# First group's Q, K and V in 480, 480, 512 and 448 columns in place of 480 four times, and one more split load at the end

## The chip, the cores and the metric

The kernel runs on one core of a Trainium2 chip. The metric is the time of one execution on the device, in microseconds. The kernel before takes 623.56 us, the median of three runs (623.55 to 623.58). A core has a matrix engine (TensorE, PE in the profile, with its weight loads as PEld), a vector engine (VectorE, DVE), a scalar engine (ScalarE, ACT), GpSimd (POOL) and a queue engine (SyncE, SP) that here does nothing but issue transfers (DMAs). Matrix products accumulate in banks of PSUM and are copied to SBUF, the memory that the engines work from.

## The reference

An input `x` of 2048 tokens by 640 is normalised per token. The result goes through two branches: local dilated attention (32 heads of 20, each token looks at itself and the seven tokens 2, 4, ... 14 before it) and a feed-forward pair with SiLU between and behind. The two are multiplied and added to `x`. Cut to what matters:

```python
xn = _layernorm(x)                                   # 2048 x 640
qkv = xn @ wqkv                                      # 640 x 1920: Q, K, V of 640 columns each
logits = einsum(q, k at pos - 2*w, w = 0..7) * Dh**-0.5     # masked where pos - 2*w < 0
o = softmax(logits) . v at the same places
s = o @ wo                                           # 640 x 640
g = silu(silu(xn @ w1) @ w2)                         # 640 -> 1536 -> 640
out = x + s * g
```

All is fp32. The kernel gets fp32 accuracy from a faster product: each operand is split into a rounded high part and the remainder, and a product is three matmuls (high x high, low x high, high x low).

## The kernel before

**Groups and stages.** The tokens form four groups of 512 (g = 0 to 3; half of the sequence by parity of the position), each of four token tiles of 128. A group has two stages. `qkv_phase` makes Q, K and V in four *quarters* of eight heads: a quarter needs 160 columns each of Q, K and V from `wqkv`, five chunks (c = 0 to 4) of the model dimension, four token tiles and three products, which is 60 matmuls, each into one PSUM bank per token tile. The attention of a quarter runs on VectorE while TensorE goes on. `ffn_phase` makes the feed-forward pair (`up`, 15 matmuls of 512 columns for one of 12 blocks; `down`, 24 matmuls of 384 and 256 columns) and, from the second group on, the output projection `wo_phase` of the group before. `wo_last` is the last group's projection; there the residual `x` is loaded, multiplied and added by token tile, in two pieces of 384 and 256 columns, and stored.

**Widths of the quarters.** A PSUM bank holds 512 fp32 columns. In groups 1 to 3 each of the first three quarters takes 32 of the fourth's query columns along (`MORE = 32`), so the widths are 512, 512, 512 and 384. In group 0 all four are 480. `parts` (L468) says which columns of `wqkv` a unit takes, `width` (L489) how many they are, and `start` (L492) where they lie in a weight slot: 48 columns in (`QAT`) in group 0, else at 0. `evac_qkv` (L745) copies a bank out: K and V with L749, the query columns with L752, and the 32 borrowed ones into the fourth quarter's `Q` with L755.

**Weights.** A weight unit (one chunk of a quarter, or one block of `w1`, `w2` or `wo`) is loaded raw by `raw_load` (L546 for its equally spaced columns, L548 for the odd piece where it has one) into one of the borrowed buffers `xr` and `gate`. ACT copies it, rounded, into one of seven slots `w` (L581), and POOL (the first ten) or DVE (the rest) makes the remainder (L585). The chunks 0, 2 and 4 of each quarter are stored as halves in DRAM when first made (L589, `half_q`), and read back from there in later groups (L572). Their DRAM tile has the later groups' widths: so in group 0 the first three quarters store 480 columns, and the 96 that lack come from the fourth quarter's unit in three stores of 32 columns each. A slot is free for its next unit when TensorE has used it and its stores have landed.

**Order.** Instructions are not issued in the order of the code. `Weave.add` records each operation with its engine, an estimated duration, what it reads and writes, and a priority; `Weave.plan` lays out a schedule from these estimates with TensorE's order fixed, tries to close TensorE's gaps by adding order between other operations, and `emit` issues everything in the order found. Each engine then takes its own list strictly in that order, and so does SP with its transfers.

Of the kernel before, what the change touches and what calls it, by code (L numbers as in the profile page):

```python
# [11 lines left out]
AF = mybir.ActivationFunctionType  # L12
# [6 lines left out]
DC, FC = D // P, F // P  # L19
NQ = 4  # L20
HQ = H // NQ
CQ = HQ * DH
# [35 lines left out]
             ("th", 1, 1), ("sq", 2), ("th", 2, 0), ("hi", 5), ("th", 2, 1), ("sq", 3), ("th", 3, 0), ("th", 3, 1), ("hi", 6))  # L58
ON_POOL = 0, -1, 1, 3, -2, 4, -3, 2, 5, 6
BY_ACT = (0,)  # L60
IN_PARTS = 2
KEYS_FIRST = ((3, 0),)
KEYS_IN = 4.0
OUT_IN = 6.0
# [3 lines left out]
LENT0, LENT_PACE = -16.0, 12.0  # L68
QAT = 48
MORE = 32  # L70
OAT = 16
X_AT = 1.2, 6, 8
TILE_AT = 1, 1.5, 5, 6
# [19 lines left out]
class Weave:  # L93
# [21 lines left out]
    def add(self, eng, dur, fn, reads=(), writes=(), prio=0.0, lock=False, table=None, nbytes=0, more=0.0, late=0.0, at=0.0,  # L115
            spans=(), quick=0.0):
        o = Op()
        o.quick = quick
        o.eng, o.dur, o.fn, o.prio, o.lock, o.table, o.nbytes = eng, dur, fn, prio, lock, table, nbytes
        o.more, o.late, o.spans = more, late, spans  # L120
        o.seq, o.users, o.at, o.need = len(self.ops), [], at, 0
        before = set()
        for k in reads:
            if k in self.writer:
                before.add(self.writer[k])
        for k in writes:
            if k in self.writer:
                before.add(self.writer[k])
            before.update(self.readers.get(k, ()))
        for k in writes:  # L130
            self.writer[k] = o
            self.readers[k] = []
        for k in reads:
            self.readers.setdefault(k, []).append(o)
        before.discard(o)
        self.ops.append(o)
        for b in before:
            self.chain(b, o)
        return o
# [164 lines left out]
def local_attention_silu_ffn(ctx: ExitStack, tc: tile.TileContext, x, wqkv, wo, w1, w2, out):  # L304
# [26 lines left out]
    def tiles(name, n, shape, dtype=F32):  # L331
        return [sb.tile(shape, dtype, name=f"{name}{i}") for i in range(n)]

    ident = sb.tile([P, P], F32, name="ident")
    def small(name, *shape):
        return sb.tile([P, *shape], F32, name=name)


    M = [small("m0", T, HQ)]
    TH = [sb.tile([P, DC * TOK + OAT], F32R, name="th0")]  # L340
    mask, ST = small("mask", T, W), [small("st0", 2, 6)]
    TH.append(sb.tile([P, DC * TOK + OAT], F32R, name="th1"))
    M.append(small("m1", T, HQ))
    ST.append(small("st1", 2, 6))
    TL = tiles("tl", 2, [P, DC * TOK + 64], F32R)
    chunks = lambda tiles, at: [v[:, at:at + DC * TOK].rearrange("p (c n) -> p c n", c=DC) for v in tiles]
    OH, OL = chunks(TH, OAT), chunks(TL, OAT)
    TH, TL = chunks(TH, 0), chunks(TL, 0)
# [7 lines left out]
    Q = tiles("q", NQ, [P, T, CQ])  # L356
# [40 lines left out]
    def act(n, fn, reads, writes, prio, table=None, more=0.0, late=0.0, at=0.0, spans=()):  # L397
        return add("ACT", ac(n) + more, fn, reads, writes, prio, table=table, late=late, at=at, spans=spans)
# [9 lines left out]
    def dma(fn, reads, writes, nbytes, prio, dur=0.45, more=0.0, quick=0.0, at=0.0):  # L408
        add("SP", dur, fn, reads, writes, prio, nbytes=nbytes, more=more, quick=quick, at=at)
# [57 lines left out]
    first_q = NQ * DC  # L467

    def parts(i):


        _, q, c = units[i]
        cols = [(s * D + q * CQ, CQ) for s in range(3)]
        if i >= first_q:
            if q < NQ - 1:
                cols.append(((NQ - 1) * CQ + q * MORE, MORE))
            else:
                cols[0] = (q * CQ + q * MORE, CQ - q * MORE)
        return cols

    for u in units:
# [7 lines left out]
    def width(i):  # L489
        return sum(n for _, n in parts(i)) if units[i][0] == "q" else D  # L490

    def start(i):  # L492

        return QAT if i < first_q else 0

    raw_in = {}
    head = {}
# [1 line left out]
    def raw_tile(k):  # L499


        if k < DC:
            return "pr", k
        if k < early:
            s = (k - DC) % 6
            return ("xr", s) if s < 2 else ("g", s - 2)
        return "xr", k % 3

    def raw_load(k):
        i = fresh[k]  # L510
        u = units[i]
        n = width(i)
        of, s = raw_tile(k)
        raw_in[of, s] = k
        if of == "pr":
            r, kr = PRV[:, s * n:(s + 1) * n], [PRK[s]]
        elif of == "g":
            r, kr = G[:, s, :n], [("g", s, 0), ("g", s, CA)]
        else:
            r, kr = XR[s][:, :n], [("xr", s)]  # L520
        raws[i] = r, kr
        more = []
        if u[0] == "q":
            _, q, c = u
            cols, m, at = parts(i), 3, 0
            whole = wqkv[c * P:(c + 1) * P, :]
            src = whole.rearrange("p (s m) -> p s m", s=3)[:, :, q * CQ:(q + 1) * CQ]
            if i >= first_q:
                if q < NQ - 1:
                    odd, lies = cols[3], 3 * CQ  # L530
                else:
                    odd, lies, src, m, at = cols[0], 0, src[:, 1:], 2, cols[0][1]
                more.append((r[:, lies:lies + odd[1]], whole[:, odd[0]:odd[0] + odd[1]]))
            dst = r[:, at:at + m * CQ].rearrange("p (s m) -> p s m", s=m)
        elif u[0] == "w1":
            src = w1.rearrange("(c p) f -> p c f", p=P)[:, :, u[1] * P:(u[1] + 1) * P]
            dst = r.rearrange("p (c f) -> p c f", c=DC)
        else:
            m = wo if u[0] == "wo" else w2
            src, dst = m[u[1] * P:(u[1] + 1) * P, :], r  # L540
        if k in BY_ACT:
            add("ACT", 0.65, lambda: nc.scalar.dma_start(dst, src), [], kr, -1, nbytes=n * P * 4)
            return

        def go():
            nc.sync.dma_start(dst, src)  # L546
            for to, by in more:
                nc.sync.dma_start(to, by)  # L548
        dma(go, [], kr, n * P * 4, 1 + k if k < 2 * DC else clock[0] + 5, (0.62 if k < 2 * DC else 0.45) * (1 + len(more)))

    def raws_due(i, k):

        while rawn[0] < len(fresh) and fresh[rawn[0]] <= i + RAW_AHEAD and raw_in.get(raw_tile(rawn[0]), -1) <= k:
            raw_load(rawn[0])
            rawn[0] += 1

    def w_load():
# [5 lines left out]
        n = width(i)  # L563
        r = WR[s]
        at = start(i)
        both = r.rearrange("p (s d) -> p s d", s=2)[:, :, at:at + n]
        whi, wlo = both[:, 0], both[:, 1]
# [9 lines left out]
        if not k:  # L577
            raw_load(0)
            rawn[0] = 1
# [7 lines left out]
        if what[i] == "store":  # L587
            def keep(to, a, b, key):
                dma(lambda: nc.sync.dma_start(to, both[:, :, a:b].bitcast(F32)), [kh, kl], [key], 2 * (b - a) * P * 4,  # L589
                    due + 25)  # L590
# [4 lines left out]
            keep(kept[:, :, :n - past], past, n, ("half", u))  # L595
            for k in range(past // MORE):
                v = ("q", k, u[2])
                keep(halves[v][:, :, 3 * CQ:], k * MORE, (k + 1) * MORE, ("half", v, "more"))
        raws_due(i, k)

    def w_next(*want):

        i = used[0]
        assert units[i] == want and i < loaded[0], (units[i], want)
        used[0] += 1
        s, n, at = i % RING, width(i), start(i)
        return WR[s][:, at:at + n], WR[s][:, D + at:D + at + n], ("wh", s), ("wl", s)
# [134 lines left out]
    def q_keys(q, t):  # L742
        return [("q", q, t)] + [("q", q, t, k) for k in range(q if q == NQ - 1 else 0)]

    def evac_qkv(g, q, t, ps, kp):  # L745
        kv, qq = KV[q], Q[q]
        skip = MORE * q if g and q == NQ - 1 else 0
        n = CQ - skip
        act(2 * CQ, lambda: nc.scalar.activation(  # L749
            kv[:, :, HALO + t, :], ps[:, n:n + 2 * CQ].rearrange("p (s m) -> p s m", s=2), AF.Copy),  # L750
            [kp], [(k, q, t) for k in ("kv", "own", "val")], -1 if (g, q) in KEYS_FIRST else 0)
        act(n, lambda: nc.scalar.activation(qq[:, t, skip:], ps[:, :n], AF.Copy), [kp],  # L752
            [("q", q, t)] if skip else q_keys(q, t), 0)
        if g and q < NQ - 1:
            act(MORE, lambda: nc.scalar.activation(  # L755
                Q[NQ - 1][:, t, q * MORE:(q + 1) * MORE], ps[:, 3 * CQ:], AF.Copy), [kp], [("q", NQ - 1, t, q)], 0)

    def halo(g, q):
        h, par = groups[g]
# [184 lines left out]
    def qkv_phase(g, i, io):  # L944
# [10 lines left out]
        for q in range(NQ):  # L955
# [26 lines left out]
            for t in range(T):  # L982
                evac_qkv(g, q, t, *ps[t])
# [94 lines left out]
    def wo_last(g, i):  # L1078
# [10 lines left out]
        for t in range(T):  # L1089
            for cs in ((A,), (B,)) if t < IN_PARTS else ((A, B),):  # L1090
                at = slice(cs[0].start, cs[-1].stop)
# [153 lines left out]
    slot = 0  # L1245
    for g in range(NG):
# [3 lines left out]
        if g < NG - 1:  # L1250
            slot = other
# [30 lines left out]
```

## Time and profile before

| | |
|---|---|
| median of 3 runs | 623.56 us (623.55 to 623.58) |
| the profiled execution's own time | 624.1 us |
| its span on the core | 622.3 us |
| granted TensorE clock | 1.0 of full speed |
| first group's first stage, TensorE | to 60.85 us |
| transfers, mean rate over the span | 269 GB/s |
| transfers issued by SP's hardware queue | 52.8% of 16 engines' span |

The span runs from the first to the last event on the core, and the execution's own time holds some 1.8 us around it. A row of a timeline gives the start, the duration, the engine, the line, the operation, what is written and read with its shape, and in brackets how long the engine sat idle before it and what ended that. In a row of windows stand the stretch, its length, then the busy time and the number of instructions, the granted clock, the busy share of the transfer engines and their rate; with one engine chosen only its busy time is shown. In the waits view a row reads: engine, what it was about to do, what it waited for, and then microseconds in total, times, and the longest.

### The profile page before, as it was taken

To read this page: it belongs to the slowest core of one execution; us is meant where nothing else is said; L and a number is where in the kernel's file an instruction comes from. 1 tells how busy PE (TensorE), PEld (TensorE's weight loads), DVE (VectorE), ACT (ScalarE), POOL (GpSimd) and SP (SyncE) were. 2 spreads that over 40 slices of the span, in tenths; PEclk is the share of its full clock that TensorE was granted. 3 is DMA by queue.
4 is the path that set the end of the run, shared out by engine and by line. 5 is a ranking of instruction groups with operands and counts; after the bars stand their busy time and mean duration, and the time that the engine had idled before them with its cause. 6 is when DMAs were issued, how large, how long until landed. Compare 5 with 4: busy or idle time off the path is not lost.

```text
span 622.3 us, 9038 instructions
## 1 busy us (share of the span) xinstructions
PE 617.2 (99%) x3395; PEld 557.9 (90%) x3395; DVE 540.7 (87%) x545; ACT 272.7 (44%) x496; POOL 114.8 (18%) x165
## 2 busy tenths in 40 slices
PE   9999999999999999999999999999999999999997
PEld 7888999998889998999888999989988999999997
DVE  6599899999788998998948499899996999899834
ACT  5445555364545225453545521625654272252220
POOL 5800000011110142111221015121222211111100
PEclk9999999999999999999999999999999999999999
DMA  9999999599999999965999999998499999987552
GB/s 297 305 319 317 323 377 364 220 326 269 278 298 309 331 237 321 272 198 140 203 219 262 344 363 330 295 230 252 137 225 286 240 321 304 295 241 243 189 191 86
DMA packets 105114, 167.39 MB, mean 269 GB/s; under 512 B 36605, under 2 KB 66781, under 8 KB 105069
## 3 DMA queue, kind: packets, MB, share of 16 engines
q1 hardware_dynamic: 78573, 87.08, 52.8%
q0 software_dynamic: 25952, 79.31, 46.6%
q8 instruction: 27, 0.44, 0.3%
q10 hardware_dynamic: 544, 0.41, 0.2%
q14 instruction: 18, 0.15, 0.1%
HBM read 107.91 MB, written 34.16 MB: 228 GB/s over the span
## 4 chain that ended last, share of the span: by engine, by line
PE 98%; DMA 0%; DVE 0%; issue 0%
PE acc L1016 22%; PE acc L1018 15%; PE acc L973 10%; PE acc L971 10%; PE acc L972 10%; PE rot L1144 9%; PE rot L1145 9%; PE rot L1143 9%; PE acc L909 2%; PE rot L644 1%; DMA xin<-in_A_x_dram 0%; PE rot L893 0%; PE rot L1129 0%; DVE st L878 0%; PE rot L852 0%; DVE gate L1097 0%
## 5 line engine op out<-in xcount | busy, mean ns | idle before, releaser
L1016 PE MATMUL acc<-w,sh 128*128 128x384 f32 x384 | 113.4, 334 | 0.0
L971 PE MATMUL acc<-w,th 128*128 128x512 f32 (+2 forms) x300 | 112.9, 376 | 0.0
L973 PE MATMUL acc<-w,th 128*128 128x512 f32 (+2 forms) x300 | 112.8, 376 | 0.0
L972 PE MATMUL acc<-w,tl 128*128 128x512 f32 (+2 forms) x300 | 112.8, 376 | 0.0
L1018 PE MATMUL acc<-w,sh 128*128 128x256 f32 x384 | 107.3, 279 | 0.0
L792 DVE TENSOR_TENSOR pr<-q,kv 128x2560 f32<-128x2560 f32 x32 | 90.3, 2822 | 16.0 <-DMA kv<-kv 15.7
L826 DVE TENSOR_TENSOR pr<-q,kv 128x2560 f32<-128x2560 f32 x32 | 94.5, 2954 | 0.7
L1143 PE MATMUL rot<-th,w 128*128 128x512 f32 x240 | 94.2, 393 | 0.0
L1145 PE MATMUL rot<-th,w 128*128 128x512 f32 x240 | 93.8, 391 | 0.0
L1144 PE MATMUL rot<-tl,w 128*128 128x512 f32 x240 | 93.7, 391 | 0.0
L795 DVE TENSOR_REDUCE l<-pr 128x128 f32<-128x2560 f32 x32 | 90.1, 2815 | 0.3
L1156 ACT ACTIVATE sh<-rot 128x512 fp32r<-128x512 f32 x48 | 28.8, 600 | 139.7 <-PE rot L1145 139.5
L572 POOL DMA_DIRECT2D w<-half_q x52 | 37.4, 719 | 234.4 <-DVE pr L831 97.2
L572 POOL DMA_DIRECT2D w<-half_w x72 | 38.6, 536 | 202.7 <-PE acc L1018 87.9
L831 DVE TENSOR_TENSOR pr<-pr 128x1280 f32<-128x1280 f32 x64 | 74.0, 1156 | 1.3
L1018 PEld LDWEIGHTS acc<-w,sh 128*128 128x128 f32 x384 | 72.2, 188 | 1.1 <-DVE gate L1048 0.3
L1016 PEld LDWEIGHTS acc<-w,sh 128*128 128x128 f32 x384 | 72.1, 188 | 0.9
L972 PEld LDWEIGHTS acc<-w,tl 128*128 128x128 f32 x300 | 56.3, 188 | 8.8
L973 PEld LDWEIGHTS acc<-w,th 128*128 128x128 f32 x300 | 56.3, 188 | 8.7
L971 PEld LDWEIGHTS acc<-w,th 128*128 128x128 f32 x300 | 56.3, 188 | 8.7
L1016 PE MATMUL acc<-w,sl 128*128 128x384 f32 x192 | 57.9, 333 | 0.0
L749 ACT ACTIVATE kv<-acc 128x320 f32<-128x320 f32 x64 | 27.5, 441 | 60.9 <-PE acc L973 59.5
(115 smaller groups left out, 1037.8 us busy)
## 6 DMA issues: line engine op xcount, KB each, us to landing
w<-half_w POOLq DMA_DIRECT2D x72, 640.0 KB, 6.6
w<-half_q POOLq DMA_DIRECT2D x39, 512.0 KB, 5.5
half_w<-w SPq DMA_DIRECT2D x24, 640.0 KB
kv<-kv SPq DMA_DIRECT2D x15, 560.0 KB
w<-half_wo POOLq DMA_DIRECT2D x10, 640.0 KB, 8.0
kv<-kv SPq DMA_DIRECT2D x15, 420.0 KB
gate<-in_B_w_dram SPq DMA_DIRECT2D x16, 320.0 KB
w<-half_q POOLq DMA_DIRECT2D x13, 384.0 KB, 7.6
```

Of the source, the lines that this page charges most:

```text
L572: add("POOL", 1.0, lambda: nc.gpsimd.dma_start(both, src), [("half", u), ("half", u, "more")], [kh, kl], due + 10, nbytes=2 * n * P * 4)
L792: dve(2560, lambda t=t: nc.vector.tensor_tensor(out=PR, in0=win(qq[:, t:t + 2, :], W, 0), in1=win(kv[:, 0, t:t + 2, :], W, CQ), op=OP.mult ...
L795: dve(2560, lambda t=t: nc.vector.tensor_reduce(out=l[:, t:t + 2].rearrange("p t w h -> p (t w h)"), in_=PR.rearrange("p t w (h d) -> p (t ...
L826: dve(2560, lambda t=t, v=v: nc.vector.tensor_tensor(out=PR.rearrange("p t w (h d) -> p t (w h) d", d=DH), in0=e[:, t:t + 2].rearrange("p ...
L971: nc.tensor.matmul(o, hi, wh, start=c == 0, stop=False)
L972: nc.tensor.matmul(o, lo, wh, start=False, stop=False)
L973: nc.tensor.matmul(o, hi, wl, start=False, stop=c == DC - 1)
L1016: nc.tensor.matmul(a[t][0][:, :CA], st, w[:, :CA], start=first, stop=last)
L1018: nc.tensor.matmul(b[t // 2][0][:, h * CB:(h + 1) * CB], st, w[:, CA:], start=first and h == 0, stop=last, skip_group_check=True)
L1143: nc.tensor.matmul(h, wh[:, cs], TH[i][:, c, :], start=c == 0, stop=False)
L1144: nc.tensor.matmul(h, wh[:, cs], TL[i][:, c, :], start=False, stop=False)
L1145: nc.tensor.matmul(h, wl[:, cs], TH[i][:, c, :], start=False, stop=c == DC - 1)
```

## The change

The first group's third quarter takes 32 of the fourth's query columns along, so that its width is 512 and the fourth's 448. `SLOT` renumbers the places: the third quarter's 32 columns are the first of the fourth's 160, the first and second quarter's (from group 1 on) come behind them. `start` now puts units at 48 only for the first two quarters, and the third and fourth lie at 0. A stored third quarter is whole when stored, and the fourth quarter's unit has two 32-column stores to make in place of three. Apart from that `IN_PARTS` goes from 2 to 3: in `wo_last` the residual of three token tiles, not two, is loaded in two pieces.

```diff
-IN_PARTS = 2
+IN_PARTS = 3
@@
 MORE = 32
+SLOT = 1, 2, 0
@@ parts
         cols = [(s * D + q * CQ, CQ) for s in range(3)]
-        if i >= first_q:
-            if q < NQ - 1:
-                cols.append(((NQ - 1) * CQ + q * MORE, MORE))
-            else:
-                cols[0] = (q * CQ + q * MORE, CQ - q * MORE)
+        if q == NQ - 1:
+            gone = MORE * (NQ - 1 if i >= first_q else 1)
+            cols[0] = (q * CQ + gone, CQ - gone)
+        elif i >= first_q or q == NQ - 2:
+            cols.append(((NQ - 1) * CQ + SLOT[q] * MORE, MORE))
         return cols
@@ start
-        return QAT if i < first_q else 0
+        return QAT if i < 2 * DC else 0
@@ raw_load
-            if i >= first_q:
+            if len(cols) > 3 or q == NQ - 1:
@@ evac_qkv
-        skip = MORE * q if g and q == NQ - 1 else 0
+        skip = MORE * (q if g else 1) if q == NQ - 1 else 0
@@
-        if g and q < NQ - 1:
+        if q < NQ - 1 and (g or q == NQ - 2):
+            slot = SLOT[q]
             act(MORE, lambda: nc.scalar.activation(
-                Q[NQ - 1][:, t, q * MORE:(q + 1) * MORE], ps[:, 3 * CQ:], AF.Copy), [kp], [("q", NQ - 1, t, q)], 0)
+                Q[NQ - 1][:, t, slot * MORE:(slot + 1) * MORE], ps[:, 3 * CQ:], AF.Copy), [kp], [("q", NQ - 1, t, slot)], 0)
```

The change adds two lines near the top, so a line number is up to two higher after it than before. TensorE's list has the same instructions in the same order; only the widths of 120 matmuls differ. The other engines' lists move in a few places.

SP's queue while the first group's second quarter is being made; `xr` and `gate` are the raw buffers, `kv_93` the first quarter's keys and values, which are shifted between partitions. Before:

```order
L546 DMA xr_108<-in_A_wqkv_dram 128x3x160
L767 DMA kv_93<-kv_93 112x2x480
L767 DMA kv_93<-kv_93 14x2x480
L546 DMA gate<-in_A_wqkv_dram 128x3x160 x2
L546 DMA xr_107<-in_A_wqkv_dram 128x3x160
L546 DMA gate<-in_A_wqkv_dram 128x3x160
L775 DMA carry_121<-kv_93 2x2x640
L546 DMA gate<-in_A_wqkv_dram 128x3x160
```

After:

```order
L549 DMA xr_108<-in_A_wqkv_dram 128x32
L769 DMA kv_93<-kv_93 112x2x480
L769 DMA kv_93<-kv_93 14x2x480
L547 DMA gate<-in_A_wqkv_dram 128x3x160
L549 DMA gate<-in_A_wqkv_dram 128x32
L547 DMA gate<-in_A_wqkv_dram 128x2x160
L549 DMA gate<-in_A_wqkv_dram 128x128
L547 DMA xr_107<-in_A_wqkv_dram 128x2x160
L549 DMA xr_107<-in_A_wqkv_dram 128x128
L547 DMA gate<-in_A_wqkv_dram 128x3x160
L549 DMA gate<-in_A_wqkv_dram 128x32
```

Each load of the third quarter (128x3x160) is followed by its 32 columns, each of the fourth's is two transfers (128x2x160 and 128x128), and the third quarter's last chunk, the load before the last row, now stands behind two units of the fourth.

ACT around the fourth quarter's evictions (`kv_96` and `q_100` from the banks `acc`) and the first SiLU pair (`sh_84` and `sf` from `rot_119`); `w_75` to `w_81` are the seven weight slots. Before:

```order
L749 ACTIVATE kv_96<-acc_116 128x2x160
L752 ACTIVATE q_100<-acc_116 128x160
L581 ACTIVATE w_79<-gate 128x640
L581 ACTIVATE w_76<-gate 128x640
L1156 ACT_TABLE_LOAD
L1156 ACTIVATE sh_84<-rot_119 128x512
L1157 ACTIVATE sf<-rot_119 128x512
L581 ACTIVATE w_78<-xr_108 128x640
```

After:

```order
L582 ACTIVATE w_76<-gate 128x640
L582 ACTIVATE w_79<-gate 128x640
L750 ACTIVATE kv_96<-acc_113 128x2x160
L753 ACTIVATE q_100<-acc_113 128x128
L750 ACTIVATE kv_96<-acc_114 128x2x160
L753 ACTIVATE q_100<-acc_114 128x128
L750 ACTIVATE kv_96<-acc_115 128x2x160
L753 ACTIVATE q_100<-acc_115 128x128
L750 ACTIVATE kv_96<-acc_116 128x2x160
L753 ACTIVATE q_100<-acc_116 128x128
L582 ACTIVATE w_78<-xr_108 128x640
L1158 ACT_TABLE_LOAD
```

The copies into slots 76 and 79 moved from behind the evictions to ahead of them, and the one into slot 78 from behind the first SiLU pair to ahead of it.

## The prediction

> **What bounds the kernel now.** I read the page first (busy shares, then the chain that ended last), then the waits of TensorE's weight loads, then TensorE's groups by shape, and last the stretches in which one shape runs alone.
>
> ```profile
> PE 617.2 (99%) x3395; PEld 557.9 (90%) x3395; DVE 540.7 (87%) x545; ACT 272.7 (44%) x496; POOL 114.8 (18%) x165
> PE 98%; DMA 0%; DVE 0%; issue 0%
> PEld rot L865 <- POOL ident masks.py:199: 1.4, 1, 1.4
> PEld acc L1018 <- DVE gate L1048: 0.3, 1, 0.3
> ```
>
> TensorE is busy for 617.2 of 622.3 us and is 98% of the chain. Past the start its weight loads wait for another engine only for some tenths of a microsecond. So the time is the sum of the spacings of 3395 matmuls, and an edit on another engine matters only where it makes TensorE wait. A matmul's own duration (about 380 ns) overlaps the next one's, so the price of one is the distance from start to start, which I take from stretches with one shape:
>
> ```profile
> L971 PE MATMUL acc<-w,th 128*128 128x480 f32 x60 | 22.7, 378 | 0.0
> 21.97:34.93 12.96, 12.96 (x62) 1.00 1.08 276
> 34.93:47.89 12.96, 12.96 (x62) 1.00 1.08 317
> 47.89:60.85 12.96, 12.96 (x62) 1.00 1.10 316
> 296.80:337.64 40.84, 40.84 (x182) 33.78 (x181) 29.71 (x25) 19.85 (x46) 10.59 (x15) 1.00 1.32 218
> 337.64:348.07 10.43, 10.43 (x62) 10.39 (x61) 8.33 (x11) 6.02 (x15) 0.00 (x0) 1.00 1.20 296
> ```
>
> In a group's first stage each quarter is 60 matmuls (5 chunks of the model dimension, 4 token tiles, 3 products; the counts in brackets include neighbours that reach into the stretch). The first three windows are quarters 2, 3 and 4 of the first group: 12.96 us / 60 = 216.0 ns at 480 columns. The fourth is three quarters of the third group: 40.84 / 180 = 226.9 ns at 512. The fifth is its last quarter: 10.43 / 60 = 173.8 ns at 384. The granted clock is 1.00 in all of them.
>
> **The change part by part.** *Widths.* The number of matmuls and of columns stays (480 + 480 + 512 + 448 = 4 x 480), so a cost proportional to columns changes nothing. But the three widths aren't on a line: from 384 to 512 it rises by (226.9 - 173.8) / 128 = 0.415 ns a column, which puts 480 at 213.6, and 480 costs 216.0, 2.4 ns above it. The change takes 120 matmuls off that width: 60 go to 512, whose price stands in the rows, and 60 to 448, a width that the trace lacks. Its bounds: above, 216.0, since 32 columns fewer shouldn't cost more; below, as far under the line as 480 is over it, 200.4 - 2.4 = 198.0. I take the line, 200.4, since both its ends are measured and it lies between; the chord from 384 to 480 would give 201.9. The sum for quarters 3 and 4 is 60 x (226.9 + 200.4 - 2 x 216.0) = -0.28 us, with ends of -0.43 (198.0) and +0.65 (216.0).
>
> The Trainium skill, in TensorE: Matmul & The Clock Gate, section Back-to-back issue gap, gives a warm matmul a gap of its columns / 2.4 plus 2.5 ns. That is a line in the columns, and by it the sum is zero: it speaks against the change. The trace has its slope (0.415 against 1 / 2.4 = 0.417) but a larger constant (13.5 ns at 512), and at 480 it leaves the line.
>
> *Loads and stores in SP's queue.* Each of the third quarter's five weight loads gets a second transfer of 32 columns, each of the fourth's is split in two, and three of the nine 32-column stores go away: 7 issues more.
>
> ```profile
> 11.11 0.93 SPq L548 DMA_DIRECT2D xr<-in_A_wqkv_dram  x1
> 24.55 1.10 SPq L546 DMA_DIRECT2D xr<-in_A_wqkv_dram  x1
> 27.36 1.45 SPq L546 DMA_DIRECT2D gate<-in_A_wqkv_dram  x2
> 32.53 2.18 SPq L589 DMA_DIRECT2D half_q<-w  x3
> 33.32 0.61 ACT L581 ACTIVATE w<-gate 128x480 fp32r<-128x480 f32 x1 [1.70 <-DMA gate<-in_A_wqkv_dram]
> 37.43 0.61 ACT L581 ACTIVATE w<-gate 128x480 fp32r<-128x480 f32 x1 [0.68 <-DMA half_q<-w]
> 45.51 0.38 PE L972 MATMUL acc<-w,tl 128*128 128x480 f32 x1
> ```
>
> A second issue costs 0.93 us at most (L548's row) and about 0.6 otherwise. The one that is latest in PE's sense is the last chunk of the third quarter. By the order it now stands behind three 32-column issues of its quarter and four transfers of the fourth's, so it is issued some 4 to 5 us later, near 33 us. A load issued at 27.36 was there at 33.32, so this one lands near 39; with its copy on ACT (0.61) and its remainder on DVE, even behind one 2.8 us product, it is ready by 43.5. TensorE comes to it at 34.93 + 48 x 0.227 = 45.8 us (45.3 before, just ahead of the last row). About 2 us are left: nothing on the path, and each microsecond beyond them would be one of TensorE's. DVE, which takes these in a fixed order, may come out of it some 2 us late.
>
> ```profile
> 74.82 0.82 DVE L585 TENSOR_TENSOR w<-gate,w 128x640 fp32r<-128x640 f32 x1 [1.99 <-ACT w L581]
> 152.51 0.68 DVE L694 TENSOR_TENSOR tl<-turn,th 128x512 fp32r<-128x512 f32 x1
> 155.79 0.39 PE L972 MATMUL acc<-w,tl 128*128 128x512 f32 x1
> ```
>
> That lateness has a wait of 1.99 us at 74.82 to disappear in; what comes through would meet the second group's last input chunk, done at 153.19 and read at 155.79, with 2.6 us to spare. Nothing.
>
> *Evictions.* Four ACT copies of 32 columns more, 0.20 us each by this row, and the fourth quarter's are 32 columns shorter. ACT is at 44%; nothing by itself.
>
> ```profile
> 488.26 0.20 ACT L755 ACTIVATE q<-acc 128x32 f32<-128x32 f32 x1
> 62.59 0.74 ACT L581 ACTIVATE w<-gate 128x640 fp32r<-128x640 f32 x1 [0.29 <-DMA half_q<-w]
> 64.65 0.60 ACT L1156 ACTIVATE sh<-rot 128x512 fp32r<-128x512 f32 x1
> 65.14 0.59 ACT L1157 ACTIVATE sf<-rot 128x512 f32<-128x512 f32 x1
> 65.62 0.74 ACT L581 ACTIVATE w<-xr 128x640 fp32r<-128x640 f32 x1
> 67.69 0.39 PE L1143 MATMUL rot<-th,w 128*128 128x512 f32 x1
> ```
>
> *ACT's new order.* Five copies of feed-forward weights now stand ahead of the fourth quarter's evictions, and the copy that ran at 65.62 stands ahead of the first SiLU pair. Each waits until its slot's stores have landed, and ACT takes nothing past it. Late next would be the pair (64.65 and 65.14, done at 65.73): TensorE reuses its bank at 67.69, so 1.96 us of cover stand there. The stores are also issued earlier by the new order, since three fell out. I cost it at nothing and keep the loss as a rival.
>
> *Third output tile's residual in two loads.*
>
> ```profile
> 548.31 21.96 SPq L1092 DMA_DIRECT2D xin<-in_A_x_dram  x6
> 590.70 0.33 SPq L1072 DMA_DIRECT2D pr<-in_A_x_dram  x1
> 614.45 0.56 DVE L1097 TENSOR_TENSOR gate<-acc,gate 128x384 f32<-128x384 f32 x1 [1.21 <-PE acc L1016]
> ```
>
> Six issues become seven. They are over by 570.27, 20 us ahead of SP's next, and the tile is first touched at 614.45, where DVE waits for TensorE and not for a load: nothing. The orders that the planner changed near 505 us move two remainders of the attention output earlier and put one SiLU remainder behind them; all have their TensorE readers after 510 us, as before.
>
> *The sum* is -0.28 us. Against the profiled execution: span 622.3 to 622.0. The median of the runs, 623.56, lies 1.26 above that span, and this offset stays: 623.56 - 0.28 = 623.28, say **623.3 us**.
>
> **The rivals.**
>
> ```profile
> 375.99:387.04 11.05, 11.01 (x74) 10.75 (x73) 10.98 (x11) 2.19 (x3) 7.35 (x9) 1.00 1.08 353
> 397.25:407.58 10.33, 10.33 (x73) 10.33 (x72) 10.19 (x7) 4.08 (x5) 1.59 (x3) 1.00 1.17 226
> 374.33 3.14 DVE L1048 TENSOR_TENSOR gate<-acc,gate 128x384 f32<-128x384 f32 x6
> ```
>
> (1) *The one inner wait goes.* Two stretches of the same 72 matmuls take 11.05 and 10.33 us; the first holds the 0.3 us wait for L1048 of the waits view, and after it the spacing stays wider to the stretch's end. L1048 ran from 374.33 to 377.47 behind an unbroken row of DVE work. If a shifted load brings that work 0.3 us forward, the whole 0.72 goes: 623.3 - 0.7 = 622.6. Against it: nothing in the third group is edited, and DVE there hangs on events that move along with TensorE.
>
> (2) *Columns are all that counts,* the excess at 480 being carried over to the new pair: if 448 costs 216.0 x 2 - 226.9 = 205.1, within its bounds, the sum is zero and the time 623.56. For it: two of three prices do lie where a line would have them. Against it: the only odd width measured is the one that is left.
>
> (3) *Slower: ACT's head of line at 62 to 68 us.* The copy that now precedes the SiLU pair needs the fourth quarter's 32-column stores of its slot. Those are issued by 61.75 at the latest before; with a landing of 4.9 us (issued 32.53, waited for until 37.43) that is 66.6, then copy 0.74, table load 1.28 and the pair 1.1: 69.8 against TensorE's 67.69, a stall of 2.1 us. It decides from the point where SP's additional issues push these stores past about 59.7 us. Halfway, 1.0 us, gives 623.3 + 1.0 = 624.3; the full price 625.4. For it: SP's queue is the one that the change lengthens. Against it: the stores move forward in SP's order.
>
> **How the numbers follow.** Forecast 0.60, (1) 0.10, (2) 0.12, (3) 0.18. The likeliest gives 623.3, by its own bounds 623.1 to 623.5. The range takes in (1) at its foot and (3) halfway, **622.5 to 624.6**; left out are the dear half of (3) and what nobody listed. A change of 0.2%, 1.25 us, is what the measurement can surely tell from none, that is under 622.31 or over 624.81. Below needs (1) and something besides: 0.05. Above needs more than 1.5 us of (3), or 448 at its upper end together with (3): 0.09. Within: 0.86.
>
> **What would show it.** In the profile after: quarters 3 and 4 of the first group as stretches of 13.6 us at 512 columns and 12.0 at 448 (25.64 against 25.92), the second quarter still 12.96; 448's spacing near 200 ns decides between the forecast and (2). The wait for L1048's like still there near 377 with the wide spacing behind it; if it is gone, (1). No wait of TensorE between 43 and 70 us; one on a bank that the SiLU pair frees near 67.5 would be (3). The last DVE pair of the tail still released by TensorE. The forecast is wrong if 448 costs over 204 ns, or if TensorE stalls by over 0.3 us where it doesn't in the trace of before.

## The result, and the profile after

| | before | after |
|---|---|---|
| median of 10 runs each, taken side by side | 623.62 us | 627.31 us |
| lowest and highest | 623.44, 624.48 | 624.97, 630.34 |
| the profiled execution's own time | 624.1 us | 626.98 us |
| its span | 622.3 us | 625.1 us |

The ratio is 1.0058, with a 95% interval of 1.0045 to 1.0072: the change makes the kernel slower by 0.6%. The forecast was 623.3, in a range of 622.5 to 624.6. Here and below a median is over all runs, while a ratio leaves out the few slow ones, which took over 1.5% more than the fastest of their kernel (two in e3, one in each of e1, e6 and e11, two of the kernel before).

The page of the kernel after, its busy shares and the first line of its chain of waits:

```profile
PE 616.9 (99%) x3395; PEld 557.1 (89%) x3395; DVE 538.0 (86%) x545; ACT 271.7 (43%) x500; POOL 114.6 (18%) x165
PE 90%; DMA 4%; SPq 2%; DVE 1%; ACT 1%; issue 0%; ACTq 0%; DVEq 0%
```

TensorE is as busy as before (616.9 against 617.2 us), so its work hasn't become dearer. But the chain was 98% PE and is 90% now: some stretches of it run through transfers, SP and ACT. The waits of TensorE's weight loads, after, say where they come out (what it was about to do, what it waited for, us in total, times, longest):

```profile
PEld rot L1145 <- ACT sf L1159: 2.1, 1, 2.1
PEld rot L867 <- POOL ident masks.py:199: 1.4, 1, 1.4
PEld acc L973 <- ACT q L757: 1.4, 1, 1.4
PEld rot L895 <- DVE xin L885: 0.9, 2, 0.7
PEld acc L911 <- ACT w L582: 0.5, 1, 0.5
```

The second row is the start, which was there before. The first and the third are new, and both end with ACT: one on a bank that the first SiLU pair frees (L1159), one on a bank that the third quarter's evictions free (L757). The row for L1048 near 377 us has gone. Stretches of the kernel after, TensorE alone (stretch, length, busy time and instructions, granted clock, share of the transfer engines, GB/s):

```profile
22.30:35.26 12.96, 12.96 (x62) 1.00 0.93 244
35.26:48.90 13.64, 13.64 (x61) 1.00 0.89 271
48.90:62.32 13.42, 12.43 (x62) 1.00 1.02 300
62.32:74.52 12.20, 10.56 (x47) 1.00 1.04 310
379.46:389.80 10.34, 10.34 (x74) 1.00 1.10 408
```

They are the first group's quarters 2, 3 and 4, its first three `up` blocks, and the stretch that took 11.05 us before. The one of them that the prediction doesn't show of the kernel before is that of the three blocks:

```profile
60.85:71.10 10.25, 10.25 (x47) 1.00 0.98 273
```

| stretch | before | after | difference |
|---|---|---|---|
| start to quarter 2 | 21.97 | 22.30 | +0.33 |
| quarter 2 (480 columns) | 12.96 | 12.96 | 0 |
| quarter 3 (480, now 512) | 12.96 | 13.64 | +0.68 |
| quarter 4 (480, now 448) | 12.96 | 13.42 | +0.46 |
| three `up` blocks | 10.25 | 12.20 | +1.95 |
| the stretch at 377 to 390 | 11.05 | 10.34 | -0.71 |

The sum is +2.7 of the span's +2.8 us. Without its stall quarter 4 would be shorter than before by about 0.8 us (it takes 12.16 in e7 below, which has none), and so the two stalls carry the loss of this execution: some 1.3 us in quarter 4 and 1.95 us in the `up` blocks.

**The first stall.** Rows of the timeline of the kernel after: SP issuing the last chunk of the fourth quarter (slot 80), ACT's copy of it with the third quarter's evictions behind, and TensorE.

```profile
42.70 0.97 SPq L547 DMA_DIRECT2D gate<-in_A_wqkv_dram  x1
43.72 2.19 SPq L549 DMA_DIRECT2D gate<-in_A_wqkv_dram  x1
...
50.02 0.58 ACT L582 ACTIVATE w<-gate 128x448 fp32r<-128x448 f32 x1 [5.73 <-DMA gate<-in_A_wqkv_dram]
50.50 0.42 ACT L750 ACTIVATE kv<-acc 128x320 f32<-128x320 f32 x1
...
51.01 0.20 ACT L757 ACTIVATE q<-acc 128x32 f32<-128x32 f32 x1
...
51.26 0.47 PE L973 MATMUL acc<-w,th 128*128 128x448 f32 x1 [0.99 <-ACT q L757]
```

The same places in the timeline of the kernel before:

```profile
38.25 0.97 SPq L546 DMA_DIRECT2D gate<-in_A_wqkv_dram  x1
...
45.54 0.61 ACT L581 ACTIVATE w<-gate 128x480 fp32r<-128x480 f32 x1 [4.36 <-PE acc L973]
46.15 0.44 ACT L749 ACTIVATE kv<-acc 128x320 f32<-128x320 f32 x1
```

The copy into slot 80 stands on ACT ahead of the third quarter's evictions in both kernels. Before, its load was issued at 38.25 and had long landed when the copy came up: what released the copy was TensorE. After, nine more transfers stand ahead of it in SP's list (five pieces of the third quarter, four of the fourth), so it is issued 4.45 us later, and it has a second piece itself, issued at 43.72 and landed just before 50.02. The evictions start 4.35 us later than before, and TensorE, which wants the first of those banks at 51.26 - 0.99 = 50.27, finds it full.

**The second stall.** The chain of the kernel after in order of time (start, us, what), from the store of slot 76 to TensorE:

```profile
56.43 5.58 DMA half_q<-w
...
62.08 0.75 ACT w L582
...
62.85 0.83 DVE w L586
63.69 0.09 SPq L547
...
63.82 3.86 DMA half_q<-w
...
67.75 0.74 ACT w L582
...
68.51 1.28 ACT L1158
...
69.81 0.60 ACT sh L1158
70.40 0.50 ACT sf L1159
...
70.95 0.50 PE rot L1145
```

Read it upwards. TensorE waits for the SiLU pair, the pair for the copy into slot 78 ahead of it on ACT, the copy for the last 32-column store of slot 78 (issued 63.82, landed 67.68). Ahead of that store on SP stands a raw load (L547), which went out when DVE had done with its buffer; DVE had waited for the copies at 62.08, and these for a store of slot 76 (issued 56.43). In this chain two landings stand in a row, tied together by one load. The load's wait is only a small part of the lateness, though: the whole row took 0.66 us on SP (63.11 to 63.77), and e6 below has the same stall with a load there that waits for nothing. Before, SP had all stores of slot 78 in one row, over by 61.75:

```profile
59.06 2.69 SPq L589 DMA_DIRECT2D half_q<-w  x4
```

### The profile page after: what moved, and what is told of

Same layout as the page of the kernel before. It is cut to its first block, busy times and chain, and to the rows that moved or that the text cites. A ratio compares the mean times of both kernels' runs of the same rounds, so it can differ in the third digit from the quotient of the medians.

```text
span 625.1 us, 9052 instructions
## 1 busy us (share of the span) xinstructions
PE 616.9 (99%) x3395; PEld 557.1 (89%) x3395; DVE 538.0 (86%) x545; ACT 271.7 (43%) x500; POOL 114.6 (18%) x165
## 4 chain that ended last, share of the span: by engine, by line
PE 90%; DMA 4%; SPq 2%; DVE 1%; ACT 1%; issue 0%; ACTq 0%; DVEq 0%
PE acc L1018 22%; PE acc L1020 15%; PE rot L1145 8%; PE rot L1146 8%; PE rot L1147 8%; PE acc L975 8%; PE acc L974 8%; PE acc L973 8%; PE acc L911 2%; DMA half_q<-w 2%; DMA kv<-kv 1%; DMA gate<-in_A_wqkv_dram 1%; SPq L547 1%; DMA pr<-in_A_wqkv_dram 1%; PE rot L645 1%; ACT w L582 1%
## 5 line engine op out<-in xcount | busy, mean ns | idle before, releaser
L973 PE MATMUL acc<-w,th 128*128 128x512 f32 (+3 forms) x300 | 113.0, 377 | 1.0 <-ACT q L757 1.0
L975 PE MATMUL acc<-w,th 128*128 128x512 f32 (+3 forms) x300 | 112.8, 376 | 0.0
L974 PE MATMUL acc<-w,tl 128*128 128x512 f32 (+3 forms) x300 | 112.8, 376 | 0.0
L794 DVE TENSOR_TENSOR pr<-q,kv 128x2560 f32<-128x2560 f32 x32 | 90.3, 2821 | 10.2 <-DMA kv<-carry 5.4
L828 DVE TENSOR_TENSOR pr<-q,kv 128x2560 f32<-128x2560 f32 x32 | 91.8, 2870 | 0.7
L1145 PEld LDWEIGHTS rot<-th,w 128*128 128x128 f32 x240 | 45.1, 188 | 10.8 <-ACT sf L1159 2.1
```

The costliest lines, as they stand in the source:

```text
L794: dve(2560, lambda t=t: nc.vector.tensor_tensor(out=PR, in0=win(qq[:, t:t + 2, :], W, 0), in1=win(kv[:, 0, t:t + 2, :], W, CQ), op=OP.mult ...
L828: dve(2560, lambda t=t, v=v: nc.vector.tensor_tensor(out=PR.rearrange("p t w (h d) -> p t (w h) d", d=DH), in0=e[:, t:t + 2].rearrange("p ...
L973: nc.tensor.matmul(o, hi, wh, start=c == 0, stop=False)
L974: nc.tensor.matmul(o, lo, wh, start=False, stop=False)
L975: nc.tensor.matmul(o, hi, wl, start=False, stop=c == DC - 1)
L1145: nc.tensor.matmul(h, wh[:, cs], TH[i][:, c, :], start=c == 0, stop=False)
```

## The experiments

Each line gives the medians, those of the kernel before from runs on the same chip. The ratio is an estimate from the runs with its interval, and not the quotient of the two medians. "Near 50" and "near 70" are TensorE's waits in the one profiled execution of each, as the weight loads show them; another execution of the same kernel can have others.

| kernel | median, us | before there | ratio (95% interval) | near 50 | near 70 |
|---|---|---|---|---|---|
| e1: before, residual in three tiles | 624.75 | 623.77 | 1.0008 (0.9988 to 1.0029) | 0 | 0 |
| e2: after, residual in two tiles | 626.67 | 623.77 | 1.0041 (1.0025 to 1.0057) | 0 | 2.5 |
| e8: before, no offset of 48 | 624.10 | 623.77 | 1.0002 (0.9991 to 1.0013) | 0 | 0 |
| e3: after, evictions first | 627.85 | 624.03 | 1.0042 (1.0018 to 1.0066) | 0 | 2.4 |
| e4: after, SiLU pair first | 625.38 | 624.03 | 1.0014 (0.9997 to 1.0031) | 0 | 0 |
| e5: after, both first | 625.27 | 624.03 | 1.0021 (1.0001 to 1.0040) | 0 | 0.3 |
| e6: after, one load a chunk | 625.74 | 624.03 | 1.0008 (0.9991 to 1.0026) | 0 | 1.9 |
| e7: e5 and e6 together | 623.96 | 623.77 | 0.9999 (0.9990 to 1.0008) | 0 | 0 |
| e9: before, split loads | 625.89 | 624.06 | 1.0043 (1.0025 to 1.0061) | 1.0 | 0.7 |
| e11: before, ACT's new order | 633.10 | 623.63 | 1.0103 (1.0051 to 1.0155) | 0 | 0 |
| e12: after, stores ahead of loads | 625.57 | 623.97 | 1.0036 (1.0009 to 1.0063) | 1.8 | 0 |
| e13: e6 and e12 together | 623.77 | 623.70 | 1.0002 (0.9993 to 1.0011) | 0 | 0 |

### Which part of the change it is

e1 is the kernel before with the residual's part alone; e2 is the kernel after without it.

```diff
 e1, on the kernel before
-IN_PARTS = 2
+IN_PARTS = 3
 e2, on the kernel after
-IN_PARTS = 3
+IN_PARTS = 2
```

> The kernel before with the third residual tile in two loads and nothing else of the change. Theories A and B: 623.6, no difference. Rival C (the split of the last loads costs it): about 627.

> The changed kernel with the residual loads as before (two tiles in pieces): the widths alone. Theories A and B: 625 to 630 as the whole change, median near 627.3. Rival C: 623.5.

e2 keeps the loss (+2.9 us) and the wait on the SiLU pair, the longest in this list; e1 shows neither wait. So the widths' part carries it. The wait near 50 us is absent from e2's profile, although SP's list up to there is that of the kernel after: its copy into slot 80 starts at 48.06, in place of 50.02. So the first stall is not in every execution. e1's own median lies 1.0 above that of before, its interval includes none, and what takes longer in its profile is the part behind the start of the last matmul (4.66 us to the span's end, 3.83 before). With three tiles too that part takes 3.8 us in the kernel after and in e4, and 4.2 in e7 and e13, which lie level with the kernel before; so a price of some tenths is neither shown nor excluded.

e8 asks whether 480 columns are dear because they lie 48 columns into their slot.

```diff
-QAT = 48
+QAT = 0
```

> The kernel before with the first group's weights at 0 in their slots and not 48 columns in; no engine's order changes. It asks whether the 2.4 ns by which 480 columns lie above the line belong to the width or to the place. Width: the second to fourth quarters stay at 216.0 ns a matmul (12.96 us each), time 623.6. Place: 213.6 ns, 12.82 us each, and about 0.5 us less in all.

Its quarters 2 to 4 take 39.00 us from 22.54 to 61.54, 39.00 / 180 = 216.7 ns a matmul, against 216.0 with the offset: the 2.4 ns above the line belong to the width and not to its place.

### ACT's order

The next three put back the order of before on ACT, at one place or at both: the copy into slot 80 behind the third quarter's evictions and those into 76 and 79 behind the fourth's (e3), the copy into slot 78 behind the first SiLU pair (e4), and both (e5).

```diff
 e3, in evac_qkv, behind the last eviction of a quarter
+        if g == 0 and t == T - 1:
+            for k in {2: (19,), 3: (22, 25)}.get(q, ()):
+                wv.chain(last, head["hi", k])
 e4, in the up blocks, behind the SiLU pair
+        if g == 0 and f == 0:
+            wv.chain(pair, head["hi", 24])
```

> The changed kernel, with one order more: ACT's copy of the fourth quarter's last weight chunk comes behind the third quarter's evictions and not ahead of them. Theory A (ACT takes its list in order, so evictions and the SiLU pair stand behind weight copies that wait for transfers): the wait of 1.35 us near 50 us is gone, the one near 69 us stays, some 626.0 us. Theory B (SP's longer queue is the cause by itself, whoever stands where on ACT): TensorE waits all the same, for the weights themselves at about 58 us, and the time stays near 627.3.

> The changed kernel, with ACT's feed-forward weight copies put behind the fourth quarter's evictions (two of them) and behind the first SiLU pair (one). Theory A: the wait near 69 us (2.0 us) is gone, the one near 50 us (1.25 us) stays: some 625.3 us. Theory B: the stores that the copies wait for are as late as before, TensorE then waits for the weights of the second and third feed-forward blocks, and the time stays near 627.3.

> The changed kernel with both orders of the two experiments beside it. Theory A: no wait of TensorE between 40 and 75 us, 623.4 us where the wait near 377 us is still there and 622.7 where it is not; the spread of the runs shrinks from 5 us to under 1. Theory B: 626 or more.

Neither single theory held. e3's profile has no wait near 50 (its evictions start at 47.05, with no copy ahead of them), but its time is no better than that of the kernel after. Its waits view:

```profile
PEld rot L1148 <- ACT sf L1162: 2.4, 1, 2.4
```

The end of the second stall is set by the stores and not by TensorE: TensorE goes on at 69.97, in place of 70.95, so 1.0 us is won there, but as it comes earlier it waits longer, and in this execution the clock fell behind the longer wait (last section) and took the gain back. e4 takes that wait away and lies 1.35 us over the kernel before, in place of 3.69, near the 625.3 that its theory A gave; e5 lies no further down (1.24), where theory A gave 623.4 or less and theory B 626. Their profiles show only waits of 0.3 to 0.7 us, near 68 us and in the stages behind. But both profiled executions are among the fastest two of their twelve (624.01 and 624.59), and e4's shows no wait near 50, where nothing of its edit reaches; what their usual run waits for isn't seen. The order of ACT is therefore a part of it, and not shown to be all.

### SP's queue

e6 loads each chunk of the fourth quarter in one transfer, with 32 query columns that nobody uses: five issues fewer, and every other engine's list is that of the kernel after. e7 adds e5's order.

```diff
 e6, in raw_load
-            if len(cols) > 3 or q == NQ - 1:
+            if q == NQ - 1 and i < first_q:
+                r = wide_raw(of, s)
+                raws[i] = r[:, 3 * CQ - n:], kr
+            elif len(cols) > 3 or q == NQ - 1:
```

> The changed kernel with the fourth quarter's five weight loads as one transfer of 3 x 160 columns each, in place of 2 x 160 and 128; 32 of the query columns are then loaded and not used. ACT's and DVE's orders stay as they are, SP issues five transfers fewer. Theory A alone (the order costs it whatever SP does): 627.3, both waits as they are. Theory B: the last chunk lands some 2 us earlier, the wait near 50 us is gone or under 0.3 us, the one near 69 us shrinks by 1 us or more: 624 to 625.5.

> The changed kernel with the fourth quarter's weights in one transfer and with ACT's evictions and SiLU pair ahead of the weight copies: both remedies. Theories A and B: 622.6 to 623.4, no wait of TensorE between 40 and 75 us. If the widths themselves cost something that the two waits hide, over 623.6.

e6's profile has no wait near 50, as its load lands earlier (the copy into slot 80 starts at 48.64 in place of 50.02), and keeps the other one:

```profile
PEld rot L1151 <- ACT sf L1165: 1.9, 1, 1.9
```

From its chain (start, us, what): the load ahead of slot 78's last store on SP, that store until it has landed, and the copy that waits for it:

```profile
61.13 0.57 SPq L553
61.75 4.42 DMA half_q<-w
66.32 0.74 ACT w L588
```

The load goes out right behind the store before it (done at 61.02), without a wait, and the store behind it still lands only at 66.17; in e2, with its stall of 2.5, it is the same (load 60.68, store 61.48, landed 66.42). So the blocked load of the kernel after isn't needed for the second stall.

e7 has neither wait, and its time is that of the kernel before (its expectation gave 622.6 to 623.4; the gain of the widths and the missing wait near 377 us don't show in its median). As it has no stall, its quarters 2, 3 and 4 give the clean price of the widths:

```profile
21.86:34.82 12.96, 12.96 (x62) 1.00 1.08 271
34.82:48.44 13.62, 13.62 (x62) 1.00 1.06 300
48.44:60.60 12.16, 12.16 (x62) 1.00 1.09 329
```

13.62 / 60 = 227.0 ns at 512 columns and 12.16 / 60 = 202.7 at 448; together 25.78 us against 25.92 before, 0.14 less.

e9 asks the opposite: the kernel before, its widths and its order on every other engine, with the third and the fourth quarter's chunks loaded in two transfers each, which is ten issues more.

```diff
 e9, in raw_load
+            if 2 * DC <= i < first_q:
+                more.append((r[:, :CQ], whole[:, q * CQ:(q + 1) * CQ]))
+                src, m, at = src[:, 1:], 2, CQ
```

> The kernel before, all widths 480 and its order on ACT, DVE and POOL, but the first group's third and fourth quarters load each weight chunk in two transfers (K and Q or two thirds of it, then the rest): SP gets 10 issues more, nothing else changes. Theory 'both are needed' (a later landing costs only where ACT has put a copy that waits for it ahead of work that TensorE waits for): the one copy that stands ahead of the third quarter's evictions in this order too may be late, so at most a wait near 50 us, and none at 68 to 72 us, where the SiLU pair stays ahead of the copy into slot 78: 623.6 to 624.9. Theory 'SP alone' (the longer queue is enough, whatever ACT's order): the wait of some 2 us near 70 us appears here as well, 625.5 to 627. Theory 'the width of 448' (columns, not issues): nothing, 623.6 with no wait at all.

It costs 1.8 us, more than "both are needed" allowed; "SP alone" had the time right, but its wait of 2 us near 70 is 0.7 here. The waits of its weight loads:

```profile
PEld acc L974 <- ACT q L755: 1.0, 1, 1.0
PEld rot L1146 <- ACT sf L1160: 0.7, 1, 0.7
```

Both waits appear with no width changed and no row of ACT moved: the order of before has copies ahead of the third quarter's evictions (slot 80) and of the SiLU pair (76 and 79) too. They had cost nothing because what they wait for was early.

e11 tries ACT's order alone, on the kernel before.

```diff
 e11, the copies into slots 76 and 79 ahead of the fourth quarter's first eviction
+        if g == 0 and (q, t) == (NQ - 1, 0):
+            for k in (22, 25):
+                wv.chain(head["hi", k], first)
 and the copy into slot 78 ahead of the pair
+        if g == 0 and f == 0:
+            wv.chain(head["hi", 24], pair)
```

> The kernel before, with its widths and its loads, but ACT's order is made that of the change at two places: the copies into slots 76 and 79 ahead of the fourth quarter's first eviction, the copy into slot 78 ahead of the first SiLU pair. SP's list is the same up to the fourth quarter's shifts; behind them some transfers of the next stages change places. In the kernel before the copy into slot 78 ran at 65.62, right behind the pair, without a wait. Theory 'each of the two alone costs its part' (SP's queue 1.3 to 1.8 us, ACT's order some 1.7): a wait of 1 to 2 us near 69 us on the bank that the SiLU pair frees, 624.8 to 625.8, and nothing near 50 us. Theory 'SP alone' (a copy ahead costs nothing as long as its stores land as early as before): a wait of 0.5 us at most, 623.6 to 624.3.

Its median, 633.10, says nothing on the question, since the planner moved much of the later program as well, and the waits that came of it (2.9, 1.9 and 1.8 us) lie behind 180 us. Its profile does say something. ACT's timeline:

```profile
61.84 1.61 ACT L581 ACTIVATE w<-gate 128x640 fp32r<-128x640 f32 x2
...
65.08 0.60 ACT L1162 ACTIVATE sf<-rot 128x512 f32<-128x512 f32 x1
65.58 0.73 ACT L581 ACTIVATE w<-xr 128x640 fp32r<-128x640 f32 x1
66.21 0.59 ACT L1159 ACTIVATE sh<-rot 128x512 fp32r<-128x512 f32 x1
```

All three copies start without a bracket, that is without waiting, the one into slot 78 ahead of the pair's `sh`, and TensorE has no wait from 40 to 78 us. With stores as early as before (SP has all eight of slots 78 and 80 in one row from 59.15), a copy at this place costs nothing. It isn't quite the change's order: the planner put the pair's `sf` ahead of that copy, and three of the four tiles' evictions ahead of the other two.

### The two places in SP's list

`head` now also keeps the stores and the raw loads as they are recorded (25, 5 x `DC`, is the load for slot 79). e12 leaves the kernel after its number of issues and the copy into slot 78 ahead of the pair, and puts the stores of slots 76 and 78 on SP ahead of the next stage's raw loads. e13 adds e6's single loads. Neither ties an instruction of ACT to a place; the copy into slot 79 moves behind the pair together with its load.

```diff
 e12, behind the first SiLU pair
+        if g == 0 and f == 0:
+            for key in [key for key in head if key[0] == "kept" and key[1] in (3 * DC, 3 * DC + 2)]:
+                wv.chain(head[key], head["raw", 5 * DC])
```

> The kernel after, with its widths, its number of issues and its copy into slot 78 ahead of the first SiLU pair, but in SP's list the stores of slots 76 and 78 (chunks 0 and 2 of the fourth quarter) are put ahead of the next stage's raw loads, in place of one load in the middle of each; the copy into slot 79 moves behind the pair with its load. Theory 'two landings in a row' (in the change a raw load waits for the buffer that the copy into slot 76 empties, that copy waits for a store to land, and the last store of slot 78 stands behind that load on SP): the stores of 78 land by about 66 us, the copy into 78 runs without a long wait, and TensorE's wait near 69 us falls from 2.1 to under 0.7 us; what is near 50 us stays; 624.5 to 626.0. Theory 'the copy's place on ACT is enough': the wait stays at some 2 us, 626.5 to 627.5.

> The kernel after with SP's list mended in both places and ACT's list left as in e12_stores_first, no instruction of ACT pinned: the fourth quarter's weight chunks of the first group are loaded in one transfer each (160 query columns, of which 128 are used), 5 issues fewer, and the stores of slots 76 and 78 stand ahead of the next stage's raw loads. Theory 'SP is all of it': no wait above 0.5 us near 50 us or near 69 us, 623.4 to 624.4, the kernel before within its measurement. Theory 'ACT's order has a price of its own': at least one of the two waits stays, 625 to 626.

The waits of e12, the first row:

```profile
PEld acc L973 <- ACT q L757: 1.8, 1, 1.8
```

and its copy into slot 78 with the pair behind it, on ACT:

```profile
64.95 0.74 ACT L582 ACTIVATE w<-xr 128x640 fp32r<-128x640 f32 x1 [1.35 <-DMA half_q<-w]
...
67.50 0.59 ACT L1159 ACTIVATE sf<-rot 128x512 f32<-128x512 f32 x1
```

The copy still stands ahead of the pair. It starts at 64.95 in place of 67.75, the pair is done at 68.1, and no wait near 70 is left; the one near 50 is, as expected. The last 32-column store of slot 78 has landed by 64.95, in place of 67.7. In e13 both are gone. Its windows and the copy into slot 80:

```profile
35.00:48.50 13.50, 13.50 (x61) 1.00 1.05 308
48.50:61.00 12.50, 12.50 (x63) 1.00 1.05 315
61.00:72.00 11.00, 11.00 (x52) 1.00 1.04 288
```

```profile
48.14 0.58 ACT L588 ACTIVATE w<-gate 128x448 fp32r<-128x448 f32 x1 [5.43 <-DMA gate<-in_A_wqkv_dram]
```

TensorE is busy without a gap through all three. That copy still waits for its load, but ends 1.9 us earlier than in the kernel after, and that is enough. The four kernels form a square; the differences of their medians to the kernel before, in us:

| over the kernel before | load and store as in after | stores ahead of the loads |
|---|---|---|
| two loads a chunk | after: +3.69 | e12: +1.60 |
| one load a chunk | e6: +1.71 | e13: +0.07 |

By these the late load costs some 1.5 to 2.0 us, the stores behind the loads 1.6 to 2.1, and together they are the loss: e13's runs, from 623.63 to 624.94, lie level with those of before. How the loss divides is not settled. The ratios, times 623.6, give +3.6, +2.2, +0.5 and +0.1 for the same four, which is 2.1 to 3.1 for the load and 0.4 to 1.4 for the stores. The figure of e6 is the loosest: three of its twelve runs took 623.9 to 624.0 us, as if they had no stall, and its interval includes none. That the single load is needed beside the order of the stores is shown by e12, whose interval lies above 1. That the order of the stores is needed beside the single load rests on e6's median and on the wait of 1.9 in its profile.

## Why the prediction was wrong, by its own steps

**Widths.** Right in sign and in kind: 448 has a price of its own off the line's proportion, and the pair is cheaper. It was mis-sized: 448 costs 202.7 ns and not 200.4. It lies 2.4 ns above the line, just as 480 does, so half of the gain of 0.28 was there (0.14), which no median here could tell from none. Rival (2), 205.1, is off by as much on the other side.

**Loads and stores in SP's queue: the step that failed.** It said that the latest chunk "in PE's sense is the last chunk of the third quarter", and for that chunk its numbers held. Rows of the kernel after, its issue and its copy:

```profile
33.70 0.58 SPq L547 DMA_DIRECT2D gate<-in_A_wqkv_dram  x1
...
39.95 0.63 ACT L582 ACTIVATE w<-gate 128x512 fp32r<-128x512 f32 x1 [0.85 <-DMA half_q<-w]
```

Near 33 and near 39 were forecast (the copy waited last for a store, so the load had landed by then). But the step asked only when TensorE needs a chunk. The fourth quarter's last chunk isn't needed before 58 us, and so was passed over; its copy, though, stands on ACT ahead of the third quarter's evictions, which TensorE needs at 50.3. The shape of this trap was in the trace of before, where the copy at 45.54 is followed by the evictions at 46.15. Counting seven issues more also hid that ten of them come before this point and the three that fall out only behind it. e6, e9 and e13 show it.

**ACT's new order: cost at nothing, wrongly.** The mechanism was listed as rival (3), with its place right (the copy into slot 78 ahead of the pair) and its price near: 2.1 us forecast, 2.1 seen on the weight load and 1.64 as TensorE's idle time before the matmul. What sent it to the rivals was the sentence "the stores move forward in SP's order". Three stores do fall out, but of slot 78's three the last now stands behind a raw load, where before nothing stood between them, and SP comes to the three later (61.13 against 59.06): the last was issued at 63.82, where before it was out by 61.75. What was counted was rows, and not when SP comes to those that stay. The rival's own sum said more than was made of it: stores issued at 61.75, as late as before, already gave the full 2.1 us, and the term was nothing only if they came by 59.7, for which no row stood. e6 is just that case, with the store issued at 61.75 and a wait of 1.9. e12 and e13 show that the stall goes when the stores stand ahead of the loads, with the copy still ahead of the pair, so the copy's place alone isn't the cause; e11's trace agrees. How much of the lateness comes from the load's own issue, from its data on the way or from its wait isn't separated.

**What nobody listed** is that the two come together. Rival (3) at its full price gave 625.4; in the profile after, the first stall makes the rest. That the range reached to only half of (3) left it short as well.

**Rival (1)** came true in the profile after (10.34 us where there were 11.05) and takes back 0.7 us. The wait is also absent from e1, e8 and e9, which have the widths of before, and present in e5 (0.3), which has those of the change; so the widths don't decide it, and what does is open. In e5 the same 72 matmuls take 10.63 us: there the wait costs its 0.3 and no more, so the wider spacing behind it in the kernel before isn't its consequence as such, as the rival had it.

**The rest.** The evictions and the residual's third tile were costed at nothing, and no run shows a price clear of the noise. The wait of 0.5 us on the first quarter's weights (L911) and the +0.33 us at the start were not followed up; in the experiments that wait reaches from nothing to 0.7.

## What to carry to other kernels

An issue added to a queue has to be followed to every instruction that stands behind whatever waits for it, on each engine that takes its list in order: a chunk that TensorE needs late can be the one that holds up an eviction that it needs soon. In a reordered list of transfers look at what now stands ahead of a store that some engine waits for, and when the store was out before; that fewer stores are left says little. And two stalls of this kind hide each other: mending the first alone (e3) made the wait at the second longer, so try the repairs together before one of them is called useless.

## What the runs showed of the hardware

In three profiles a wait of TensorE cost more than its length. In e2 the wait on the SiLU pair left TensorE idle from about 67.5 to 69.7, and its windows then read:

```profile
70.00:72.00 2.00, 2.00 (x7) 0.59 1.12 226
72.00:74.00 2.00, 2.00 (x7) 0.55 1.05 230
74.00:76.00 2.00, 2.00 (x14) 1.00 1.12 260
```

The granted clock was 0.55 to 0.59 for some 3.5 us, with starts of the 512-column matmuls 427 ns apart in place of 227: about eight matmuls, 1.6 us on top of the wait. The same is seen in e3 behind its wait of 2.4 (0.50 from 72 to 74 us) and in e11 behind that of 2.9 (0.50 from 220 to 222). In the kernel after, the wait of 2.1 left no such mark (1.00 throughout), nor did e12's of 1.8 and e6's of 1.9. On the matmuls, from start to start less one spacing, these gaps are 2.8 us (e11), 2.2 (e2) and 2.1 (e3) against 1.8 (after), 1.6 (e6) and 1.4 (e12). So in these six stalls the edge lies between 1.8 and 2.1 us, and the kernel after sits near it. Its runs agree: the mean clock of the three that took 629.5 us or more was 0.995 to 0.997, that of the seven others (624.97 to 628.54) 0.999 or 1.0. One such dip, 3.5 of 625 us at little over half, gives 0.997 as an estimate, and e2's profiled execution has that mean.

The widths 480 and 448 both lie 2.4 ns above the line through 384 and 512. Why is open; e8 rules out the offset in the slot.
